# Strassen's algorithm in both products of two of three token blocks of a gated MoE layer, with stored operands

## The chip, the cores and the metric

The kernel runs on one core of a Trainium2 chip. The metric is the device time of one execution in microseconds, as the median of several runs. A core has a matrix engine (TensorE, PE in the profile; its weight loads are PEld), three engines for elementwise work (VectorE or DVE, ScalarE or ACT, GpSimd or POOL) and SyncE (SP), whose queue issues all DMA transfers here.

## What is computed

Linear attention over 4 batches of 576 tokens and 8 heads gives 2304 tokens of 512 features. They pass a dense layer (512 to 2048 to 512) and then four experts, all of which see every token:

```python
def _moe_ref(x, w_in, w_out):
    h = x @ w_in
    g = np.maximum(0.01 * h, h)
    return g @ w_out

def _moe2_ref(x, domain_probs, w1, w2):
    p = domain_probs / (domain_probs.sum(-1, keepdims=True) + 1e-09)
    out = np.zeros((N, D))
    for e in range(E):                       # 4 experts, w1[e] 512x1024, w2[e] 1024x512
        h = np.maximum(x @ w1[e], 0.0)
        out += p[:, e:e + 1] * (h @ w2[e])
    return out
```

All arrays are fp32.

## The kernel before

Each fp32 factor is split in a high part of a shorter type (fp32r) and the remainder; a product is three matmuls, hi·hi, hi·lo and lo·hi (`PASS`). ScalarE makes most high parts, VectorE or GpSimd subtract them for the low parts.

The attention of batch b+1 runs between the matmuls of the first layer for batch b. For the first layer VectorE splits weights and activations (`gt<-g,gt`, `wt`, L118) and adds the results up in `acc` (L551). SyncE loads the probabilities early (`load_probs`, L133) among the attention's first loads; VectorE normalises them in place (L138).

The second layer takes the tokens in NB = 3 blocks of 768 (two halves of TH = 384) and the 4096 hidden units of the four experts in NC2 = 16 chunks of 256: 48 groups, one call of `group(k)` each. A group has two parts:

- The up product of chunk k is a 2x2 block product by the Strassen-Winograd scheme: 7 products (`product`, matmul L722) of 6 matmuls with 384 columns, on sums of the weights (AOPS) and of the tokens (XOPS). They accumulate in the banks X, V and Y; two sums on VectorE (V += s1 at L824, Z = Y + s0 at L827) put the four quarters together, and ScalarE (L735) and VectorE (L739) apply the relu and split.
- The down product of chunk k−1 is conventional: six token tiles (`down`, matmul L761), each of 6 matmuls with 512 columns. VectorE multiplies each by its token's probability and adds it to the output tile `ob` (L777). After the last chunk of a block the tile is stored (L781).

The order on TensorE within a group is products 1 and 5, tile 3, products 2 and 6, tile 4, products 3 and 7, tiles 5 and 0, product 4, tiles 1 and 2. `keep_in_program_order` (by `kept`) holds it.

The weights of a chunk are loaded anew for each block (`w2_dma`, `w2_dma_d`), one group ahead. GpSimd forms the four sums of w1 (`w2_sums`, L682), ScalarE rounds (L699, L710) and GpSimd subtracts (L704 twice a group, L714 once). The token sums of block 0 are made by `x2_steps(0)` on VectorE (L619, L642) at the end of the first layer, out of `acc` in SBUF; those of blocks 1 and 2 by GpSimd during the block before.

Of the kernel before, what the change touches and what calls it, by code (L numbers as in the profile page):

```python
# [7 lines left out]
F32 = mybir.dt.float32  # L8
# [8 lines left out]
DF = 128  # L17
# [7 lines left out]
GF = 4  # L25
# [46 lines left out]
N_X = 10  # L72
# [3 lines left out]
NC2 = NE * FF2 // 256  # L76


@with_exitstack
def body(ctx, tc, kT, qT, vh, w_phi, w_in, w_out, probs, w1, w2, out):  # L80
# [3 lines left out]
    xp = ec(tc.tile_pool(name="xp", bufs=N_X))  # L84
# [19 lines left out]
    def unit(name, dt=F32):  # L104
        return up.tile([128, S], dt, tag="u", name=name)
# [125 lines left out]
    def kv_side(b, hp, h):  # L231
# [17 lines left out]
        if h == 1:  # L249
            if "n" in DIRECT[b]:  # L250
                kv = up.tile([128, 4, 128], F32, tag="u", name="kv")
# [3 lines left out]
            kvh = up.tile([128, 4, 128], F32R, tag="u", name="kvh")  # L255
            kvl = up.tile([128, 4, 128], F32R, tag="u", name="kvl")
# [235 lines left out]
    accs = {}  # L492

# [83 lines left out]

    XOPS = ("b11", "t1", "b21", "t2", "b22", "t3", "t4")
    xops = {}

    def pieces(*halves):

        cuts = sorted({0, TH} | {S - t0 % S for t0 in halves if S - t0 % S < TH})  # L590
        return [
            (o, e - o, [((t0 + o) // S, (t0 + o) % S) for t0 in halves])
            for o, e in zip(cuts, cuts[1:])
        ]

    x2p = []

    def x2_steps(j):

        T = (2 * TH * j, 2 * TH * j + TH)  # L600
        kind = ([xp, xp, xp, 0, 0], [0, xp, xp, xp, xp], [xp, xp, xp, 0, 0])[j]
        slots, raw = [], []
        xops[j] = {}

        def half(i):
            if i % 3 == 0:
                pool = kind[i // 3] or x2p[0]
                slots.append(pool.tile([128, 3, 2, TH], F32R, tag="x", name="xo"))
            return slots[i // 3][:, i % 3]

        def part(d, t, o, n):
            b, s = t
            return accs[b][:, 2 * d : 2 * d + 2, s : s + n]

        eng = nc.vector if j == 0 else nc.gpsimd

        def diff(out, f, g, halves):
            for o, n, at in pieces(*halves):
                kept(eng.tensor_tensor(  # L619
                    out=out[:, :, o : o + n], in0=f(o, n, at), in1=g(o, n, at), op=ALU.subtract  # L620
                ))

        def step(i, name):
            if name[0] == "t":
                if not raw:
                    raw.append((x2p[0] if j else xp).tile([128, 3, 2, TH], F32, tag="x", name="xt"))
                r = raw[0][:, {"t1": 0, "t2": 1, "t3": 2, "t4": 0}[name]]
                of = {
                    "t1": (lambda o, n, at: part(0, at[1], o, n), lambda o, n, at: part(0, at[0], o, n), T),
                    "t2": (lambda o, n, at: part(1, at[0], o, n), lambda o, n, at: raw[0][:, 0, :, o : o + n], T[1:]),  # L630
                    "t3": (lambda o, n, at: part(1, at[0], o, n), lambda o, n, at: part(0, at[0], o, n), T[1:]),
                    "t4": (lambda o, n, at: part(1, at[0], o, n), lambda o, n, at: raw[0][:, 1, :, o : o + n], T[:1]),
                }[name]
                diff(r, *of)
                src = [(0, TH, r)]
            else:
                d, t = int(name[1]) - 1, T[int(name[2]) - 1]
                src = [(o, n, part(d, at[0], o, n)) for o, n, at in pieces(t)]
            hi, lo = half(2 * i), half(2 * i + 1)
            for o, n, r in src:  # L640
                kept(nc.scalar.copy(out=hi[:, :, o : o + n], in_=r))
                kept(eng.tensor_tensor(  # L642
                    out=lo[:, :, o : o + n], in0=r, in1=hi[:, :, o : o + n].bitcast(F32), op=ALU.subtract
                ))
            xops[j][name] = hi, lo
# [292 lines left out]
```

## Time and profile before

| | before |
|---|---|
| median of 3 runs | 1379.31 us (1379.19 to 1380.08) |
| the profiled execution: span | 1378.8 us |
| granted TensorE clock, mean | 0.992 |
| TensorE busy | 1352.1 us (98%) |
| VectorE busy | 817.8 us (59%) |
| ScalarE busy | 657.9 us (48%) |
| GpSimd busy | 567.8 us (41%) |
| DMA traffic | 134.94 MB, mean 98 GB/s |

The span is the time from the first to the last instruction of one profiled execution; the runs are timed without a profile. Busy time is summed over an engine's instructions; that of TensorE is modelled at the ends of its matmuls, so distances between starts are more reliable than durations there. A row of a timeline gives the start, the duration, engine, line, operation, output<-input and how many instructions it joins; behind it in brackets stands the idle time ahead of it and what ended it.

### The profile page before, as it was taken

What the parts mean: (1) busy time and instruction counts of PE and PEld (TensorE: products, weight loads), DVE (VectorE), ACT (ScalarE), POOL (GpSimd) and SP (SyncE); (2) the same over time, 40 slices, a digit from 0 to 9 for tenths busy, and PEclk for the clock granted to TensorE, in tenths of its full rate; (3) what the DMA queues carried; (4) which work ended last, traced back from release to release, by engine and by line L of the source; (5) the groups of instructions that cost most, each with busy time, mean ns of one, the idle gap of its engine ahead of it and who ended that gap; (6) DMA issues with size and microseconds to landing.
All of it is one profiled execution on the core that took longest, in us unless ns stands there. A gap on an engine that the chain in (4) does not pass through costs nothing.

```text
span 1378.8 us, 21301 instructions
## 1 busy us (share of the span) xinstructions
PE 1352.1 (98%) x8105; PEld 1262.2 (92%) x8105; DVE 817.8 (59%) x1285; ACT 657.9 (48%) x1201; POOL 567.8 (41%) x398
## 2 busy tenths in 40 slices
PE   8979999999999999999999999999999999999998
PEld 6778999999999999998999999999999999899997
DVE  4589999678786656553555445445454444554444
ACT  5657657676576435424343443434443343433331
POOL 3211102111111000027767666767767675565651
PEclk9989999999999999999999999999999999999999
DMA  6466645333332222302212122321121232122111
GB/s 220 113 217 234 220 167 166 111 120 105 109 103 66 75 86 73 104 24 94 75 61 77 62 68 71 107 77 62 62 77 62 77 107 77 62 64 76 61 62 62
DMA packets 78518, 134.94 MB, mean 98 GB/s; under 512 B 12240, under 2 KB 22608, under 8 KB 78416
## 3 DMA queue, kind: packets, MB, share of 16 engines
q1 hardware_dynamic: 78416, 133.58, 29.8%
q8 instruction: 64, 1.05, 0.3%
q14 instruction: 38, 0.31, 0.1%
HBM read 120.30 MB, written 13.18 MB: 97 GB/s over the span
## 4 chain that ended last, share of the span: by engine, by line
PE 95%; DVE 1%; DMA 1%; issue 1%; ACT 1%; POOL 1%; SPq 0%; POOLq 0%; ACTq 0%; DVEq 0%
PE po L761 29%; PE hp L506 15%; PE op L538 14%; PE py L722 11%; PE pv L722 7%; PE px L722 7%; PE kvp L242 5%; PE nm L335 4%; PE pk L204 2%; PE pq L292 1%; PE pq L289 1%; DMA qraw<-qT 1%; POOL wul L704 0%; DMA r<-w 0%; DMA ds<-nf 0%
## 5 line engine op out<-in xcount | busy, mean ns | idle before, releaser
L761 PE MATMUL po<-wd,gh 128*128 128x512 f32 x1152 | 387.7, 391 | 0.9 <-POOL wd L714 0.9
L777 DVE SCALAR_TENSOR_TENSOR ob<-po,pe,ob 128x512 f32<-128x512 f32 x270 | 201.6, 749 | 216.6 <-PE po L761 216.6
L761 PEld LDWEIGHTS po<-wd,gh 128*128 128x128 f32 x1152 | 216.6, 188 | 42.3 <-POOL wd L714 1.3
L761 PE MATMUL po<-wd,gl 128*128 128x512 f32 x576 | 226.2, 393 | 0.0
L538 PE MATMUL op<-gt,wt 128*128 128x288 f32 x1536 | 219.9, 297 | 1.5 <-DVE gt L118 0.8
L296 POOL PARTITION_ALL_REDUCE mb<-pc x32 | 72.3, 2266 | 355.7 <-ACT pc L294 294.7
L506 PE MATMUL hp<-xh,wt 128*128 128x288 f32 x1024 | 216.2, 298 | 0.0
L538 PEld LDWEIGHTS op<-gt,wt 128*128 128x128 f32 x1536 | 207.9, 188 | 2.9 <-DVE gt L118 1.0
L506 PEld LDWEIGHTS hp<-xh,wt 128*128 128x128 f32 x1024 | 167.5, 188 | 1.0 <-ACT wt L117 0.3
L506 PE MATMUL hp<-xl,wt 128*128 128x288 f32 x512 | 151.8, 297 | 0.0
L714 POOL TENSOR_TENSOR wd<-r,wd 128x1024 fp32r<-128x1024 f32 x48 | 114.9, 2394 | 89.4 <-ACT wd L710 89.4
L722 PE MATMUL py<-xo,wuh 128*128 128x384 f32 x576 | 148.3, 339 | 0.7 <-DVE pz L827 0.7
L682 POOL TENSOR_TENSOR rs<-r 128x256 f32<-128x256 f32 x96 | 71.1, 741 | 188.8 <-DMA r<-w 188.8
L704 POOL TENSOR_TENSOR wul<-rs,wuh 128x1024 fp32r<-128x1024 f32 x48 | 115.5, 2406 | 65.9 <-ACT wuh L699 65.9
L704 POOL TENSOR_TENSOR wul<-r,wuh 128x768 fp32r<-128x768 f32 x48 | 88.8, 1851 | 85.7 <-ACT wuh L699 85.7
L761 PEld LDWEIGHTS po<-wd,gl 128*128 128x128 f32 x576 | 108.2, 188 | 15.2
L722 PEld LDWEIGHTS py<-xo,wuh 128*128 128x128 f32 x576 | 104.9, 188 | 4.6 <-DVE pz L827 1.0
L722 PE MATMUL px<-xo,wuh 128*128 128x384 f32 x384 | 98.9, 338 | 0.7 <-DVE acc L551 0.7
L722 PE MATMUL pv<-xo,wuh 128*128 128x384 f32 x384 | 99.1, 339 | 0.0
L722 PE MATMUL py<-xo,wul 128*128 128x384 f32 x288 | 97.3, 338 | 0.0
L506 PEld LDWEIGHTS hp<-xl,wt 128*128 128x128 f32 x512 | 96.3, 188 | 0.4
L807 ACT COPY py<-px 128x384 f32<-128x384 f32 x48 | 22.2, 463 | 143.4 <-PE px L722 137.3
(114 smaller groups left out, 2349.9 us busy)
## 6 DMA issues: line engine op xcount, KB each, us to landing
r<-w SPq DMA_DIRECT2D x192, 256.0 KB, 2.8
wr<-w SPq DMA_DIRECT2D x96, 256.0 KB, 2.7
qraw<-qT SPq DMA_DIRECT2D x32, 288.0 KB, 3.7
r<-w_out SPq DMA_DIRECT2D x9, 1024.0 KB, 9.0
r<-w_in SPq DMA_DIRECT2D x8, 1024.0 KB, 6.2
w<-w SPq DMA_DIRECT2D x32, 256.0 KB, 2.8
v<-vh SPq DMA_DIRECT2D x16, 480.0 KB, 4.0
kraw<-kT SPq DMA_DIRECT2D x16, 288.0 KB, 4.0
```

Source lines behind the costliest of these rows:

```text
L204: nc.tensor.matmul(o, lhsT=x[:, cs], rhs=w, start=(i == 0), stop=(i == len(P) - 1))
L242: nc.tensor.matmul(kvp[:, a * 128 : (a + 1) * 128], lhsT=lhs, rhs=v[:, c, h * D : h * D + 128], start=(c == 0), stop=(c == 4),)
L296: nc.gpsimd.partition_all_reduce(mb, pc, 128, bass_isa.ReduceOp.absmax)
L335: nc.tensor.matmul(o, lhsT=a[:, 2 * (h % 2) + j], rhs=x[:, j * HS : (j + 1) * HS], start=(j == 0 and i == 0), stop=(j == 1 and i == len(P) ...
L506: nc.tensor.matmul(hp[:, n, 0:HS], lhsT=wi[:, a, kk * 128 : (kk + 1) * 128], rhs=x[z][:, kk, n * HS : (n + 1) * HS], start=(kk == 0 and i ...
L538: nc.tensor.matmul(op[:, n, 0:HS], lhsT=wt1[1, C * GF + f][:, a, d * 128 : (d + 1) * 128], rhs=gts[C * GF + f][:, z, n * HS : (n + 1) * HS ...
L682: kept(nc.gpsimd.tensor_tensor(out=o, in0=x, in1=y, op=op))
L704: kept(nc.gpsimd.tensor_tensor(out=lo[:, at], in0=(r[:, 1:4], s)[i], in1=hi[:, at].bitcast(F32), op=ALU.subtract))
L714: kept(nc.gpsimd.tensor_tensor(out=d[:, 1], in0=r2, in1=d[:, 0].bitcast(F32), op=ALU.subtract))
L722: kept(nc.tensor.matmul(out, lhsT=ws[w][:, AOPS[a], kk * 128 : (kk + 1) * 128], rhs=xo[z][:, kk], start=first and n == 0, stop=n == 5, ski ...
L761: kept(nc.tensor.matmul(op, lhsT=(gh, gl)[z][:, 2 * f + t, q : q + 128], rhs=d[:, w, f], start=n == 0, stop=n == 5,))
L777: kept(nc.vector.scalar_tensor_tensor(out=o, in0=op, scalar=ps, in1=o, op0=ALU.mult, op1=ALU.add))
```

## The change

Block 1 of the change's name is the first block (k = 0 to 15), blocks 2 and 3 are k = 16 to 47. The first block keeps its products, their order and its output form, and stores its operands to DRAM: the split w1 sums (`wu`), the split quarters of w2 (`wp`), and sums of w2 (`wx`), which are new: VectorE adds them (`ws_sums`, four operations of 128x256 per group) and subtracts their high parts (`ws_lo`), ScalarE rounds. In all 3.67 MB are stored per group.

```diff
     def w2_lo(k, r, s, i):
...
+        if i:
+            d = drw.tile([128, 7, 2, 256], F32, name=f"wu_{k}")
+            for z, t in ((0, hi), (1, lo)):
+                nc.sync.dma_start(out=d[:, :, z], in_=t.bitcast(F32))
+            wd[0, k] = {n: d[:, q] for q, n in enumerate(AOPS)}
...
+            (2, r2[:, 2], r2[:, 0], ALU.subtract),
+            (3, r2[:, 3], s[:, 1], ALU.subtract),
+        ):
+            kept(nc.vector.tensor_tensor(out=s[:, o], in0=x, in1=y, op=op))
...
+    def ws_lo(k):
+        hi, lo = wsd.pop(k)
+        h, s = hi.bitcast(F32), lo.bitcast(F32)
+        kept(nc.vector.tensor_tensor(out=lo, in0=s, in1=h, op=ALU.subtract))
+        t = drw.tile([128, 4, 2, 256], F32, name=f"wx_{k}")
+        for z, x in ((0, h), (1, s)):
+            nc.sync.dma_start(out=t[:, :, z], in_=x)
...
     def group(k, r, r2, fill):
...
         product(k, 2, X, False)
         relu_hi(k, 0, X)
         relu_lo(k, 0, X)
+        ws_sums(k, r2)
         product(k, 6, Y, False)
```

The output of the first layer is stored to DRAM (`x2_0` to `x2_3`) and loaded again by `x2_steps`, whose elementwise work is now all GpSimd's, 11 operations of 128x768 for a block, with 7 ScalarE roundings. For the first and second block it runs during the last batch of the first layer (`spread(x2_steps(0), B - 0.95, B - 0.5) + spread(x2_steps(1), B - 0.5, B - 0.05)`), for the third in twelve chunks of the second block.

The probabilities are laid out expert by expert and, once normalised, also stored transposed, so that `p_load` can fetch a row of them to all partitions:

```diff
+        pT.append(drw.tile([NE, NTOK], F32, name="pT"))
+        nc.sync.dma_start(out=pT[0].rearrange("e (c p) -> p e c", p=128), in_=pe)
```

The second and third block are written as a list of steps with times (`moe2_plan`, 14 units a chunk). Up products of chunk k and down products of chunk k−1 alternate, seven each. The hidden layer is kept with hidden units on partitions and tokens on columns, gated by the probabilities at once (`gate`), and the down product takes the same seven-product scheme: four differences on GpSimd (`gsum`), seven roundings on ScalarE (`ghi`), seven subtractions on GpSimd (`glo`), 7 × 6 matmuls of 384 columns, each product added to its own accumulator `ac` of 128x768 (`evict`). Operands come by 14 loads of 256 KB per chunk (`w_load`), issued nine to eleven products ahead. After the last chunk of a block seven additions between accumulators (`plus`) give the four output quarters, which are stored transposed.

```diff
+    def down_product(k, p):
+
+        i, a, b = DOWN[p]
+        t = po[k, i] = m2["po"].tile([128, 2, 512], F32, tag="o", name="po")
+        w, g = wo[1, k, a], go[k, b]
+        for m in range(2):
+            for n, (wz, z) in enumerate(PASS):
+                kept(nc.tensor.matmul(
+                    t[:, m, 0:TH],
+                    lhsT=w[:, wz, m * 128 : (m + 1) * 128],
+                    rhs=g[:, z],
...
+    def evict(k, p):
...
+            kept(nc.vector.tensor_tensor(out=A[j, i], in0=src, in1=A[j, i], op=ALU.add))
...
+                for p in range(7):
+                    at(B + 2 * p, up_product, k, p)
...
+                for p in range(7):
+                    at(B + 2 * p + 1, down_product, k - 1, p)
+                    at(B + 2 * p + 2.0, evict, k - 1, p)
+            if k > KA + 1 and k % NC2 == 1:
+                j = k // NC2 - 1
+                for t, a, b in ((2.2, 2, 1), (4.2, 6, 1), (6.2, 7, 6), (8.2, 6, 5),
+                                (10.4, 5, 7), (12.2, 3, 6), (14.2, 4, 7)):
+                    at(B + t, plus, V, j, a, b)
...
+        for t, e, a, b in (
+            (6.2, V, 6, 1), (4.2, V, 3, 5), (2.2, V, 2, 1), (6.4, V, 3, 6), (8.2, V, 7, 6),
+            (8.3, G, 4, 7), (8.4, V, 5, 7),
+        ):
+            at(B + t, plus, e, j, a, b)
```

The scheduler decides where instructions outside `kept` stand. At three places the order is as follows. The first is SyncE's queue at the program's start (`qraw` and `kraw` are the attention's queries and keys, `w_in` and `w_out` the first layer's weights). Before:

```order
L133 DMA pe<-probs 128x72
L166 DMA qraw<-qT 128x576 x2
L154 DMA kraw<-kT 128x576
L166 DMA qraw<-qT 128x576 x3
L445 DMA r_207<-w_in 128x2x1024
L445 DMA r_209<-w_out 128x2x1024
```

After, in the same place:

```order
L142 DMA pe<-probs 128x72
L181 DMA qraw<-qT 128x576 x2
L169 DMA kraw<-kT 128x576
L181 DMA qraw<-qT 128x576
L153 DMA pT<-pe 128x72x1
L181 DMA qraw<-qT 128x576 x2
L460 DMA r_210<-w_in 128x2x1024
L460 DMA r_212<-w_out 128x2x1024
```

The store of the probabilities, which waits for VectorE, now stands ahead of two query loads and of the first weights.

The second is VectorE in one group of the first block (`gl` the relu's low part, `ob` an eviction, `pv` and `pz` the two sums). Before:

```order
L739 SCALAR_TENSOR_TENSOR gl<-px,gh 128x384
L777 SCALAR_TENSOR_TENSOR ob<-po,pe,ob 128x512
L824 TENSOR_TENSOR pv<-pv,s 128x384
L827 TENSOR_TENSOR pz<-py,s 128x384
L739 SCALAR_TENSOR_TENSOR gl<-pv,gh 128x384
L739 SCALAR_TENSOR_TENSOR gl<-pz,gh 128x384
```

After (`wsl` are the sums of w2, `r_7632` is w2 as loaded):

```order
L794 TENSOR_TENSOR wsl<-wsl,wsh 128x1024
L869 SCALAR_TENSOR_TENSOR ob<-po,pe,ob 128x512
L831 SCALAR_TENSOR_TENSOR gl<-px,gh 128x384
L783 TENSOR_TENSOR wsl<-r_7632 128x256
L783 TENSOR_TENSOR wsl<-wsl,r_7632 128x256
L783 TENSOR_TENSOR wsl<-r_7632 128x256
L783 TENSOR_TENSOR wsl<-r_7632,wsl 128x256
L869 SCALAR_TENSOR_TENSOR ob<-po,pe,ob 128x512
L918 TENSOR_TENSOR pv<-pv,s 128x384
L921 TENSOR_TENSOR pz<-py,s 128x384
```

Four sums now stand between the relu step of X and the eviction and the two sums behind it, and one subtraction of 128x1024 earlier.

The third is the end of VectorE's queue. Before:

```order
L739 SCALAR_TENSOR_TENSOR gl<-py,gh 128x384
L777 SCALAR_TENSOR_TENSOR ob<-po,pe,ob 128x512 x8
```

After, from the last gate on:

```order
L984 SCALAR_TENSOR_TENSOR b_15192<-py,pb 128x384
L1029 TENSOR_TENSOR ac<-po,ac 128x768 x2
L1032 TENSOR_TENSOR ac<-ac 128x768
L1029 TENSOR_TENSOR ac<-po,ac 128x768
L1032 TENSOR_TENSOR ac<-ac 128x768
L1029 TENSOR_TENSOR ac<-po,ac 128x768
L1032 TENSOR_TENSOR ac<-ac 128x768 x2
L1029 TENSOR_TENSOR ac<-po,ac 128x768
L1032 TENSOR_TENSOR ac<-ac 128x768 x2
L1029 TENSOR_TENSOR ac<-po,ac 128x768 x3
```

Six additions between accumulators stand between the eight last evictions; the seventh is on GpSimd.

## Rows read from the trace of the kernel before

**Rows 1.** The page: busy times, and the chain that ended last.

```profile
PE 1352.1 (98%) x8105; PEld 1262.2 (92%) x8105; DVE 817.8 (59%) x1285; ACT 657.9 (48%) x1201; POOL 567.8 (41%) x398
PE 95%; DVE 1%; DMA 1%; issue 1%; ACT 1%; POOL 1%; SPq 0%; POOLq 0%; ACTq 0%; DVEq 0%
```

**Rows 2.** TensorE's waits after 560 us, first and last of five: total, times, longest.

```profile
PE po L761 <- POOL wd L714: 0.9, 1, 0.9
...
PE py L722 <- DVE pz L827: 0.7, 1, 0.7
```

**Rows 3.** TensorE's timeline in the first block of the second layer.

```profile
645.11 0.39 PE L761 MATMUL po<-wd,gh 128*128 128x512 f32 x1
...
647.86 0.51 PE L722 MATMUL px<-xo,wuh 128*128 128x384 f32 x2
...
663.50 0.51 PE L722 MATMUL px<-xo,wuh 128*128 128x384 f32 x2
```

**Rows 4.** The timeline's end, all engines.

```profile
1374.59 0.39 PE L761 MATMUL po<-wd,gh 128*128 128x512 f32 x1
...
1375.02 0.75 DVE L777 SCALAR_TENSOR_TENSOR ob<-po,pe,ob 128x512 f32<-128x512 f32 x1 [0.61 <-PE po L761]
```

**Rows 5.** VectorE's groups by shape, 100 to 620 us: busy, mean ns, idle before.

```profile
L642 DVE TENSOR_TENSOR xo<-xt,xo 128x768 fp32r<-128x768 f32 x4 | 3.7, 950 | 1.0 <-ACT xo L641 1.0
...
L619 DVE TENSOR_TENSOR xt<-acc 128x384 f32<-128x384 f32 x4 | 2.0, 552 | 0.0
```

**Rows 6.** GpSimd's groups by shape, whole span.

```profile
L619 POOL TENSOR_TENSOR xt<-acc,xt 128x768 f32<-128x768 f32 x3 | 5.5, 1840 | 0.0
...
L619 POOL TENSOR_TENSOR xt<-acc 128x384 f32<-128x384 f32 x2 | 2.0, 1014 | 0.0
```

**Rows 7.** One line of VectorE from 500 to 600 us; then timelines of VectorE and GpSimd.

```profile
L118 DVE TENSOR_TENSOR gt<-g,gt 128x576 fp32r<-128x576 f32 x16 | 12.1, 759 | 2.3
...
610.67 1.87 DVE L118 TENSOR_TENSOR gt<-g,gt 128x576 fp32r<-128x576 f32 x1 [0.74 <-ACT gt L117]
...
609.52 2.41 POOL L704 TENSOR_TENSOR wul<-rs,wuh 128x1024 fp32r<-128x1024 f32 x1
```

**Rows 8.** Timelines of TensorE and GpSimd in the second layer's first group.

```profile
622.49 0.62 PE L722 MATMUL px<-xo,wuh 128*128 128x384 f32 x2 [0.68 <-DVE acc L551]
...
628.05 1.83 POOL L704 TENSOR_TENSOR wul<-r,wuh 128x768 fp32r<-128x768 f32 x1
629.83 2.42 POOL L704 TENSOR_TENSOR wul<-rs,wuh 128x1024 fp32r<-128x1024 f32 x1
```

**Rows 9.** Timelines of TensorE, VectorE and GpSimd in a later group.

```profile
882.42 0.52 PE L722 MATMUL px<-xo,wuh 128*128 128x384 f32 x2
...
887.68 0.56 DVE L739 SCALAR_TENSOR_TENSOR gl<-px,gh 128x384 fp32r<-128x384 f32 x1 [0.82 <-ACT gh L735]
...
886.08 1.85 POOL L704 TENSOR_TENSOR wul<-r,wuh 128x768 fp32r<-128x768 f32 x1 [2.57 <-ACT wuh L699]
889.72 2.41 POOL L704 TENSOR_TENSOR wul<-rs,wuh 128x1024 fp32r<-128x1024 f32 x1 [1.79 <-ACT wuh L699]
...
894.23 0.51 PE L722 MATMUL py<-xo,wuh 128*128 128x384 f32 x2
```

**Rows 10.** The start: SyncE, ScalarE, one transfer's landing, and a stretch of small packets.

```profile
10.80 0.38 SPq L445 DMA_DIRECT2D r<-w_in  x1
...
25.37 1.22 ACT L460 ACTIVATE w<-r 128x512 f32<-128x512 f32 x2
...
r<-w_in SPq DMA_DIRECT2D x8, 1024.0 KB, 6.2
...
35.50:35.75 0.25, 0.25 (x5) 0.25 (x4) 0.25 (x1) 0.25 (x2) 0.00 (x0) 1.00 0.37 19
```

**Rows 11.** DMA: the page's queue row, and a stretch (last columns clock, DMA share, GB/s).

```profile
q1 hardware_dynamic: 78416, 133.58, 29.8%
...
100.00:200.00 100.00, 98.10 (x688) 93.17 (x687) 94.52 (x166) 70.31 (x142) 9.84 (x4) 1.00 0.64 226
```

More of the change, by code (lines that the diff above doesn't have):

```diff
@@ L576, in moe1_group @@
         return M
[L585 to L645, printed above, removed]
-        return [lambda i=i, name=name: step(i, name) for i, name in enumerate(XOPS)]
@@ new lines, in body, with xo_load, w_load @@
+    xo = {}
+    def xo_load(m):
+        j, i = divmod(m, 7)
+        name = XOPS[i]
+        pool, tag = (m2["te"], "te") if m % N_XO < N_XE else (m2["tx"], "tx")
+        hl = [pool.tile([128, 2, TH], F32R, tag=tag, name="xo2") for _ in range(2)]
+        for z in range(2):
+            kept(nc.sync.dma_start(out=hl[z].bitcast(F32), in_=xod[j][name][:, z]))
+        xo[j, name] = hl
+    wo = {}
+    def w_load(i, n):
+        k, p = divmod(n, 7)
+        k += KA
+        name = (UP, DOWN)[i][p][1]
+        if i:
+            pool, tag = (m2["w2e"], "w2e") if n % N_W2 < N_W2E else (m2["w2"], "w2")
+        else:
+            pool, tag = m2["w1"], "w1"
+        t = pool.tile([128, 2, 256], F32R, tag=tag, name="wo")
+        kept(nc.sync.dma_start(out=t.bitcast(F32), in_=wd[i, k % NC2][name]))
+        wo[i, k, name] = t
@@ L812, in group @@
             w2_lo(k + 1, r, s, 0)
+        if k:
+            ws_lo(k - 1)
         run(down(k - 1, 3))
@@ L840, in group, with p_load, up_product @@
         run(down(k - 1, 2))
+    pb = {}
+    def p_load(j, e):
+        t = m2["p"].tile([128, 2, TH], F32, tag="p", name="pb")
+        src = pT[0][e : e + 1, 2 * TH * j : 2 * TH * (j + 1)]
+        kept(nc.sync.dma_start(
+            out=t.rearrange("p a s -> p (a s)"), in_=src.to_broadcast([128, 2 * TH])
+        ))
+        pb[j, e] = t
+    banks = {}
+    gr, go, sv = {}, {}, {}
+    def up_product(k, p):
+        i, a, b = UP[p]
+        if i == 1:
+            banks["x"] = m2["px"].tile([128, 512], F32, tag="x", name="px")[:, 0:TH]
+        if i == 5:
+            banks["v"] = m2["pv"].tile([128, 512], F32, tag="v", name="pv")[:, 0:TH]
+        out = banks[{1: "x", 2: "x", 5: "v", 3: "v"}.get(i, "y")]
+        w, x = wo[0, k, a], xo[k // NC2, b]
+        first = i in (1, 5)
+        n = 0
+        for kk in range(2):
+            for wz, z in PASS:
+                kept(nc.tensor.matmul(
+                    out,
+                    lhsT=w[:, wz, kk * 128 : (kk + 1) * 128],
+                    rhs=x[z][:, kk],
+                    start=first and n == 0,
+                    stop=n == 5,
+                    skip_group_check=not first,
+                ))
+                n += 1
@@ new lines, in ftile, with save, gate, gsum @@
+    def ftile(name):
+        return m2["f"].tile([128, TH], F32, tag="f", name=name)
+    def save(k, name, bank):
+        sv[name] = ftile("s")
+        kept(nc.scalar.copy(out=sv[name], in_=banks[bank]))
+    def gate(k, name, src, h):
+        j, c = divmod(k, NC2)
+        t = gr[k, name] = ftile(name)
+        kept(nc.vector.scalar_tensor_tensor(
+            out=t, in0=src, scalar=0.0, in1=pb[j, c // (NC2 // NE)][:, h],
+            op0=ALU.max, op1=ALU.mult,
+        ))
+    def gsum(k, name, a, b):
+        t = gr[k, name] = ftile(name)
+        kept(nc.gpsimd.tensor_tensor(out=t, in0=gr[k, a], in1=gr[k, b], op=ALU.subtract))
@@ new lines, in evict, with plus, store @@
+    def evict(k, p):
+        i = DOWN[p][0]
+        j, c = divmod(k, NC2)
+        src = po.pop((k, i))[:, :, 0:TH]
+        if c == 0:
+            A[j, i] = m2["a"].tile([128, 2, TH], F32, tag="a", name="ac")
+            kept(nc.scalar.copy(out=A[j, i], in_=src))
+        else:
+            kept(nc.vector.tensor_tensor(out=A[j, i], in0=src, in1=A[j, i], op=ALU.add))
+    def plus(eng, j, a, b):
+        kept(eng.tensor_tensor(out=A[j, a], in0=A[j, a], in1=A[j, b], op=ALU.add))
+    def store(j, a, i, h):
+        t0 = 2 * TH * (j - 1) + TH * h
+        r = out[2 * TH * DM :].rearrange("(d s) -> d s", s=NTOK - 2 * TH)
+        nc.sync.dma_start(
+            out=r[i * 256 : (i + 1) * 256, t0 : t0 + TH].rearrange("(t p) s -> p t s", p=128),
+            in_=A[j, a],
+        )
```

379 lines of the change are left out of this document (293 added, 86 removed).

## The prediction

> **What bounds the kernel now.** I read the page first, then the chain of waits, then TensorE's own waits, then timelines of one group. The page gives TensorE 1352.1 of 1378.8 us and no other engine above 59%; the chain that ended last is 95% TensorE [rows 1]. The next view asks whether TensorE ever stands still in the second layer: after 560 us it waits five times, 0.7 to 0.9 us each, 3.8 us in all [rows 2]. So in this stage the time is the sum of its matmuls, and a change must be counted in matmuls first and in new waits second.
>
> Matmul records overlap, so I take the distance between starts. Two groups of the second layer start at 647.86 and 663.50: 15.64 us for 42 matmuls of 384 columns (seven products of six) and 36 of 512 (six token tiles of six). Twelve of the wide ones lie between 645.11 and 647.86: 0.229 us each, 8.25 us for 36. That leaves 7.39 us for the 42, 0.176 us each [rows 3].
>
> **What the change takes away.** In blocks 2 and 3 the 36 wide matmuls of a group become 42 of 384 columns: 7.39 in place of 8.25 us. A chunk is then 84 × 0.176 = 14.78 us, 0.86 us less. There are 32 such chunks: **−27.5 us**. A rule of the Trainium skill ("TensorE: Matmul & The Clock Gate", "Back-to-back issue gap") gives N/2.4 + 2.5 ns from start to start, by which 36 × 215.8 − 42 × 162.5 = 0.94 us would be saved per chunk and 30.2 us in all; the rows show some 14 ns over that on both widths, and I go by the rows.
>
> **What it adds.** Six places can make TensorE wait. Each is priced from the nearest rows, with both ends.
>
> *The end.* Today the last matmul starts at 1374.59, VectorE evicts it at 1375.02 in 0.75 us, and the last store ends the span at 1378.8 [rows 4]. Afterwards the last chunk has no up products between its down products: seven of 6 × 0.176 = 1.06 us follow each other in 7.4 us, and each needs an eviction of 128x768, then there are seven additions between accumulators. VectorE took 0.950 us for a 128x768 operation from SBUF [rows 5]; the additions are of that kind, and I take the same for the evictions. Its queue then holds 8 evictions (one left from the chunk before) and 6 additions, 14 × 0.95 = 13.3 us, 13.6 with its first semaphore, against 7.4 + 0.25 + 0.95 = 8.6 us if only the last product had to be evicted: 5.0 us. The seventh addition is GpSimd's, 1.84 us by its rows for that shape [rows 6], partly beside the others, and its store is larger. Taken **+6**, between 4 and 8. What covers today's evictions, the matmuls between them, is what is gone.
>
> *The border of blocks 2 and 3.* In one chunk VectorE has its four gates and two sums of 128x384, 6 × 0.56 = 3.4 us by a step of that width [rows 9], and seven additions of two SBUF operands, 6.7 us. That fits in 14.78. But GpSimd now has 11 subtractions of 128x384 a chunk at 1.01 us [rows 6], 11.1 us, and each addition may have to wait for one (below): 3.4 + 6.7 + 7 × 1.0 = 17.1, 2.3 us too long. Taken **+2**, 0 to 5.
>
> *GpSimd against VectorE.* At 610.67 a VectorE subtraction of 128x576 with both inputs in SBUF took 1.87 us, where the mean of its line is 0.759; a GpSimd operation ran from 609.52 to 611.93, and the slow one ended at 612.54, 0.61 us after it [rows 7]. The Trainium skill ("SBUF — State Buffer", "Who interferes with whom") says that such a VectorE instruction and a GpSimd one lock each other out; by that rule the pair behaves as these rows do. It does not touch operations with an operand in PSUM, which most of VectorE's here have.
>
> *The last block of the first layer.* The operands of blocks 1 and 2 are now made there, all on GpSimd: 22 operations of 128x768 at 1.84 us = 40.5 us [rows 6] in a stretch where VectorE's subtractions of SBUF pairs feed the matmuls. Each collision costs a VectorE step up to 1.1 us (1.87 − 0.76), mostly absorbed by operands made ahead, since TensorE hardly waits there now [rows 2]. Taken **+2**, 0 to 8.
>
> *The first groups.* Block 1 now has four VectorE sums of 128x256 per group, SBUF with SBUF. By VectorE's rows for 384 and 768 elements (0.552 and 0.950, 1.04 ns an element) one takes 0.42 us. In group 0, which starts at 622.49, GpSimd's two splits run back to back from 628.05 to 632.25 [rows 8], just where these sums come (5.8 us after the start, as next worked out): up to 3.9 us late, and the same once more before GpSimd's lead is back. Taken **+4**, 0 to 8.
>
> *The other groups of block 1.* In a settled group, which starts at 882.42, the sums stand behind the subtraction that ends at 888.24, 5.82 us in. GpSimd's first split ends at 887.93, its second starts at 889.72 [rows 9]. The last of four sums would start 1.26 us after 5.82, at 7.08, 0.22 us before the second split at 7.30. So they just fit, and a few will not. Taken **+3** over 14 groups, 0 to 8.
>
> *The start.* The gate probabilities are now stored transposed, 9216 elements of 4 bytes, 576 on each of 16 DMA engines. The packets of a window with only small ones kept the engines 0.37 × 0.25 us × 16 / 128 = 11.6 ns each [rows 10] (19 GB/s × 0.25 us is one store of 4.5 KB in 128 pieces), so 6.7 us; at the mean packet of the page, 0.298 × 16 × 1378.8 / 78416 = 84 ns [rows 11], 48 us. I take the first, since its packets are as small. In SyncE's queue the store stands ahead of two query loads and of the first expert weights, and waits for VectorE's quotient; the weights were issued at 10.80, landed 6.2 us later by the page, and are first read at 25.37 [rows 10], some 8 us of slack. Taken **+1**, 0 to 40.
>
> Everything else I cost at nothing: the loads of 256 KB and additions of blocks 2 and 3 stand nine to eleven products ahead of use, GpSimd has 11.1 to 13 us of work in a chunk of 14.78, ScalarE less. If those loads were late, TensorE would show waits on them.
>
> **Sum**, against the profiled span of 1378.8: −27.5 + 6 + 2 + 2 + 4 + 3 + 1 = −9.5, so 1369.3. The median of the runs, 1379.31, lies 0.5 above that span; I add it: **1369.8 us**.
>
> **Rivals.**
>
> *The gain comes nearly whole.* The costs of block 1 and of the start all have zero as one end; with 4 at the end and 0 to 2 at the border this gives 1379.3 − 27.5 + 4 to 6, 1356 to 1358. For it: TensorE waits so little today. Against: the end is a queue that I can count.
>
> *VectorE's sums lose to GpSimd in every group of block 1* (slower). The margin of 0.22 us is the point that decides. If the sums start only after the second split, at 889.72 + 2.41 = 892.13, they end at 893.8; behind them stand an eviction of 0.75 and the two sums of 0.57 that product 4 needs, ready at 895.7 and seen at 895.95. Product 4 starts at 894.23 today [rows 9], so TensorE waits 1.7 us, 27 us over 16 groups: 1369.8 + 27 − 7 (the terms it replaces) = 1390. Any wait above some 1.2 us a group ends slower than before. For it: rows 7 show the lock. Against: the sums come first, if barely, and are short.
>
> *The stores saturate the DMA engines in block 1* (slower at its upper end). Per group 3.67 MB are stored in pieces of 1 KB and 1.05 MB loaded: 302 GB/s, where 100 to 200 us shows 226 at a share of 0.64 [rows 11]. The page's mean packet is 133.58 MB / 78416 = 1.70 KB in 84 ns. 224 packets of 1 KB per engine take between 50 and 84 ns, 11 to 19 us, and the loads 3.2 more: 14 to 22 us against 15.64. From 55 ns on they fall behind; each further 5 ns costs 224 × 5 ns = 1.1 us a group, 18 us in 16 (1369.8 − 3 + 18 = 1385 at 60 ns, 1467 at 84 ns). Against: buffers let a store take a whole group, and the same 302 GB/s need only 0.86 of the engines at the efficiency of that stretch.
>
> *The transposed store holds up the start.* At 84 ns a packet the queries and first weights are 40 us late, less 8 of slack: 1385 to 1405.
>
> That the products would not be exchanged is excluded: the instruction counts are in the order of the program.
>
> **How the numbers follow.** Forecast 0.67 (1359 to 1377 by its bounds taken singly); whole gain 0.10; VectorE's sums late 0.08; DMA in block 1 0.10; slow start 0.05. A measurement of this kernel tells 0.2% (2.8 us) from no change. Faster holds the first two cases, less 0.02 for the forecast's upper tail, and a fifth of the DMA case: 0.77. Slower holds the sums and the start, 0.13, and half of the DMA case: 0.18. The rest, 0.05, is no change. The range of 8 in 10, 1355 to 1384, leaves out some 0.03 below and, above, what the three slow cases hold there, 0.17.
>
> **What would show it.** In the changed profile: a distance of 14.8 us from chunk to chunk in blocks 2 and 3; hardly a TensorE wait there, but 2 us in the second chunk of block 3; the last matmul some 10 us before the end in place of 4; in block 1 a period of 15.6 to 15.9 us, with waits in the first two groups named after VectorE; small packets done before 20 us. A period of over 16.5 us in block 1 would make the forecast wrong, by VectorE if its sums last over 1 us each, by DMA if a load lands last. So would a chunk above 15.2 us later on.

## The result and the profile after

The changed kernel takes 1391.28 us (median of 4 runs, 1388.83 to 1391.72) against 1379.25 us before: 1.008 times, 95% interval 1.0066 to 1.0094. It is slower by 12 us, where 1369.8 was forecast. One execution of one experiment (the sums moved, on the change) took 4633.78 us, with matmuls of 384 columns some 0.63 us apart at a granted clock of 1.00, and is left out of every time below.

| | before | after |
|---|---|---|
| span of the profiled execution | 1378.8 us | 1389.2 us |
| TensorE busy | 1352.1 us (98%) | 1332.2 us (96%) |
| VectorE busy | 817.8 us (59%) | 945.0 us (68%) |
| GpSimd busy | 567.8 us (41%) | 653.7 us (47%) |
| DMA traffic | 134.94 MB, 98 GB/s | 313.91 MB, 226 GB/s |
| mean granted clock | 0.992 | 0.982 |

TensorE has 20 us less work and a span that is 10 us longer, so it must wait some 30 us more than before. Its waits, over the whole span, longest first (total, times, longest):

```profile
PE pq L304 <- DMA qraw<-qT: 18.1, 3, 15.9
PE po L1013 <- issue: 6.4, 4, 2.3
PE py L811 <- DVE pz L921: 5.9, 1, 5.9
```

The first are query products of the attention, the longest wait of 15.9 us by the fifth of them; they wait for the queries (`qraw`). The second is in the last chunk, the third in the second layer's first group. Between 680 and 1354 us TensorE does not wait at all. To put a sum beside each, I take the starts of the first product at five borders: group 0, group 2, the first chunk of block 2, the last chunk, and the end. Before, group 0 and group 2 start at 622.49 [rows 8] and 647.86 [rows 3], the other two at:

```profile
866.82 0.52 PE L722 MATMUL px<-xo,wuh 128*128 128x384 f32 x2
...
1351.02 0.51 PE L722 MATMUL px<-xo,wuh 128*128 128x384 f32 x2
```

After, in TensorE's timeline:

```profile
644.76 0.51 PE L811 MATMUL px<-xo,wuh 128*128 128x384 f32 x2
...
675.85 0.51 PE L811 MATMUL px<-xo,wuh 128*128 128x384 f32 x2
...
894.16 1.05 PE L964 MATMUL px<-xo,wo 128*128 128x384 f32 x5
...
1353.86 0.87 PE L964 MATMUL px<-xo,wo 128*128 128x384 f32 x4
```

| stretch | before, us | after, us | difference | forecast |
|---|---|---|---|---|
| attention and first layer | 622.5 | 644.8 | +22.3 | +3 |
| groups 0 and 1 | 25.4 | 31.1 | +5.7 | +4 |
| the other 14 groups of block 1 | 219.0 | 218.3 | −0.7 | +3 |
| blocks 2 and 3 to the last chunk's start | 484.2 | 459.7 | −24.5 | −23.8 |
| last chunk and end | 27.8 | 35.3 | +7.5 | +4.3 |
| span | 1378.8 | 1389.2 | +10.4 | −9.5 |

(The first chunk of block 2 still has the conventional down product of chunk 15. So the forecast's column has 30 × −0.86 + 2 up to the last chunk's start, and the last two gains, −1.72, with the +6 of the end in the last line.) Of the 20 us between forecast and result, 19 are in the first line.

**The start.** SyncE's timeline of the changed kernel:

```profile
11.89 0.38 SPq L153 DMA_DIRECT2D pT<-pe  x1
12.31 19.72 SPq L181 DMA_DIRECT2D qraw<-qT  x2
32.07 0.43 SPq L460 DMA_DIRECT2D r<-w_in  x1
```

The store of the probabilities is issued at 11.89, and the two query loads behind it then occupy the queue for 19.72 us; the first weights, issued at 10.80 before [rows 10], follow at 32.07. TensorE meanwhile:

```profile
25.33 0.60 PE L219 MATMUL pk<-wraw,kraw 128*128 128x256 f32 x2
41.80 2.26 PE L304 MATMUL pq<-qraw,wraw 128*128 128x288 f32 x4 [15.87 <-DMA qraw<-qT]
```

The DMA view of the stretch from 11 to 45 us (KB each, us to landing):

```profile
qraw<-qT SPq DMA_DIRECT2D x3, 288.0 KB, 16.8
...
pT<-pe SPq DMA_DIRECT2D x1, 36.0 KB, 28.5
```

36 KB take 28.5 us to land. That is 49 ns for each of 576 pieces per engine, where I took 11.6. The windows (PE, PEld, DVE, ACT, POOL, clock, DMA share, GB/s) show DMA engines that are busy with hardly any bytes, and TensorE's granted clock, which falls from 1.00 to 0.50 (2.4 to 1.2 GHz) after it has stood idle:

```profile
22.00:24.00 2.00, 2.00 (x21) 2.00 (x20) 1.99 (x3) 1.24 (x2) 0.00 (x0) 1.00 1.94 1
...
30.00:32.00 2.00, 0.00 (x0) 0.00 (x0) 0.00 (x0) 0.00 (x0) 0.00 (x0) 0.50 1.27 1
```

The clock is still 0.50 when the queries are in: the four matmuls at 41.80 take 2.26 us, where the four of the query product before them, at 20.79, took 1.14.

**Groups 0 and 1.** VectorE's sums and GpSimd's splits in group 0, after; first VectorE's timeline, then GpSimd's:

```profile
650.06 0.75 DVE L783 TENSOR_TENSOR wsl<-r 128x256 f32<-128x256 f32 x1
650.85 0.84 DVE L783 TENSOR_TENSOR wsl<-wsl,r 128x256 f32<-128x256 f32 x1
651.61 2.02 DVE L783 TENSOR_TENSOR wsl<-r 128x256 f32<-128x256 f32 x1
653.56 2.56 DVE L783 TENSOR_TENSOR wsl<-r,wsl 128x256 f32<-128x256 f32 x1
...
656.50 0.55 DVE L921 TENSOR_TENSOR pz<-py,s 128x384 f32<-128x384 f32 x1
```

```profile
651.37 1.99 POOL L751 TENSOR_TENSOR wul<-r,wuh 128x768 fp32r<-128x768 f32 x1
653.31 2.52 POOL L751 TENSOR_TENSOR wul<-rs,wuh 128x1024 fp32r<-128x1024 f32 x1
```

The third sum ends 0.3 us after the first split, the fourth 0.3 us after the second; what would take 0.42 us takes 2.02 and 2.56, and TensorE waits 5.9 us for `pz`. Behind the wait its granted clock is 0.52, and 12 matmuls of 384 columns take 3.9 us instead of 2.1:

```profile
657.00:661.00 4.00, 3.89 (x12) 3.89 (x13) 2.12 (x5) 2.92 (x5) 2.41 (x2) 0.52 0.61 223
```

In a settled group of the same kernel the sums stand free:

```profile
712.76 0.41 DVE L783 TENSOR_TENSOR wsl<-r 128x256 f32<-128x256 f32 x1
...
713.88 0.42 DVE L783 TENSOR_TENSOR wsl<-r,wsl 128x256 f32<-128x256 f32 x1
```

The second split of that group starts at 714.31, 0.43 us after the last sum's start; 0.22 was forecast.

**Block 1 and the chunks.** A window of 150 us in block 1, columns as above:

```profile
700.00:850.00 150.00, 150.00 (x751) 135.15 (x750) 98.83 (x163) 66.75 (x106) 92.20 (x69) 1.00 0.97 326
```

The DMA engines are busy 0.97 of the time, and TensorE still does not wait. A chunk of block 2 takes 954.51 − 939.71 = 14.80 us (14.78 forecast):

```profile
939.71 0.51 PE L964 MATMUL px<-xo,wo 128*128 128x384 f32 x2
...
954.51 0.68 PE L964 MATMUL px<-xo,wo 128*128 128x384 f32 x3
```

**The end.** TensorE's timeline, then VectorE's:

```profile
1376.07 1.29 PE L1013 MATMUL po<-go,wo 128*128 128x384 f32 x6 [1.35 <-issue]
1379.70 1.29 PE L1013 MATMUL po<-go,wo 128*128 128x384 f32 x6 [2.34 <-issue]
1382.55 2.26 PE L1013 MATMUL po<-go,wo 128*128 128x384 f32 x6 [1.56 <-issue]
```

```profile
1375.03 0.94 DVE L1029 TENSOR_TENSOR ac<-po,ac 128x768 f32<-128x768 f32 x1
1376.00 2.72 DVE L1032 TENSOR_TENSOR ac<-ac 128x768 f32<-128x768 f32 x2
1378.65 0.95 DVE L1029 TENSOR_TENSOR ac<-po,ac 128x768 f32<-128x768 f32 x1
1379.63 1.95 DVE L1032 TENSOR_TENSOR ac<-ac 128x768 f32<-128x768 f32 x2
...
1384.91 0.96 DVE L1029 TENSOR_TENSOR ac<-po,ac 128x768 f32<-128x768 f32 x1 [1.60 <-PE po L1013]
```

Each product starts 0.1 us after an eviction ends (1375.97, 1379.60): with two bank pairs for `po`, TensorE waits for VectorE, whose evictions stand behind additions. The last product, behind the last of these waits, takes 2.26 us where those before took 1.29; the granted clock is 0.50 from 1382 to 1385 us.

### The profile page after: what moved, and what is told of

Read it like the earlier page. It is cut to its first block, busy times and chain, and to the rows that moved or that the text cites. A ratio compares the mean times of both kernels' runs of the same rounds, so it can differ in the third digit from the quotient of the medians.

```text
span 1389.2 us, 23190 instructions
## 1 busy us (share of the span) xinstructions
PE 1332.2 (96%) x8297; PEld 1284.6 (92%) x8297; DVE 945.0 (68%) x1381; ACT 643.3 (46%) x1228; POOL 653.7 (47%) x534
## 2 busy tenths in 40 slices
DMA packets 205794, 313.91 MB, mean 226 GB/s; under 512 B 29168, under 2 KB 104560, under 8 KB 205680
## 4 chain that ended last, share of the span: by engine, by line
PE 64%; POOL 12%; issue 9%; DMA 6%; DVE 5%; ACT 3%; SPq 0%; POOLq 0%; ACTq 0%; DVEq 0%
PE op L555 12%; PE hp L522 11%; PE po L851 10%; PE po L1013 7%; POOL go L999 7%; POOL t L991 5%; PE kvp L257 4%; PE py L811 4%; PE nm L350 3%; PE py L964 3%; PE px L811 2%; PE pv L811 2%; PE px L964 2%; DMA qraw<-qT 2%; PE pv L964 2%
## 5 line engine op out<-in xcount | busy, mean ns | idle before, releaser
L1029 DVE TENSOR_TENSOR ac<-po,ac 128x768 f32<-128x768 f32 x210 | 200.4, 955 | 128.6 <-PE po L1013 128.5
L1013 PE MATMUL po<-go,wo 128*128 128x384 f32 x1344 | 274.5, 339 | 6.5 <-issue 6.4
L1013 PEld LDWEIGHTS po<-go,wo 128*128 128x128 f32 x1344 | 239.5, 188 | 8.2 <-issue 7.9
L999 POOL TENSOR_TENSOR go<-t,go 128x384 fp32r<-128x384 f32 x128 | 136.8, 1081 | 20.0 <-ACT go L995 20.0
L851 PE MATMUL po<-wd,gh 128*128 128x512 f32 x384 | 130.0, 392 | 0.0
L964 PE MATMUL py<-xo,wo 128*128 128x384 f32 x576 | 117.2, 338 | 0.0
L999 POOL TENSOR_TENSOR go<-b,go 128x384 fp32r<-128x384 f32 x96 | 101.4, 1056 | 9.3 <-ACT go L995 9.3
L964 PEld LDWEIGHTS py<-xo,wo 128*128 128x128 f32 x576 | 102.5, 188 | 0.2
L869 DVE SCALAR_TENSOR_TENSOR ob<-po,pe,ob 128x512 f32<-128x512 f32 x90 | 67.3, 748 | 45.4 <-PE po L851 45.4
L126 DVE TENSOR_TENSOR wt<-wr,wt 128x512 fp32r<-128x512 f32 x96 | 74.1, 793 | 15.7 <-ACT wt L125 13.9
L851 PEld LDWEIGHTS po<-wd,gh 128*128 128x128 f32 x384 | 72.1, 188 | 13.5
```

Of the source, the lines that this page charges most:

```text
L126: nc.vector.tensor_tensor(out=lo, in0=src, in1=hi.bitcast(F32), op=ALU.subtract)
L851: kept(nc.tensor.matmul(op.rearrange("p (h m) -> p h m", h=2), lhsT=(gh, gl)[z][:, 2 * f + t, q : q + 128], rhs=d[:, w, f::2], start=n == ...
L869: kept(nc.vector.scalar_tensor_tensor(out=o, in0=op, scalar=ps, in1=o, op0=ALU.mult, op1=ALU.add))
L964: kept(nc.tensor.matmul(out, lhsT=w[:, wz, kk * 128 : (kk + 1) * 128], rhs=x[z][:, kk], start=first and n == 0, stop=n == 5, skip_group_ch ...
L999: kept(nc.gpsimd.tensor_tensor(out=t[:, 1], in0=gr[k, name], in1=t[:, 0].bitcast(F32), op=ALU.subtract))
L1013: kept(nc.tensor.matmul(t[:, m, 0:TH], lhsT=w[:, wz, m * 128 : (m + 1) * 128], rhs=g[:, z], start=n == 0, stop=n == 2,))
```

## Experiments

Theory A says that the 4-byte store costs the start. Its rival B puts the loss on the rest of what the change does before the second layer. The first three runs tell them apart.

**The store alone, in the kernel before.**

```diff
-    pe = cst.tile([128, NTOK // 128, NE], F32, name="pe")
+    pe = cst.tile([128, NE, NTOK // 128], F32, name="pe")
...
+        pT = drw.tile([NE, NTOK], F32, name="pT")
+        nc.sync.dma_start(out=pT.rearrange("e (c p) -> p e c", p=128), in_=pe)
```

> The kernel before, with only the normalised probabilities laid out by expert and stored transposed (9216 pieces of 4 bytes) as the change does it. Theory A (this store fills SyncE's queue and the DMA engines at the start, and the attention's queries come late): 1379 + 20 to 25 = 1399 to 1404 us, TensorE idle for some 15 us ahead of 42 us, waiting for qraw. Rival B (the loss of the first 650 us comes from the other parts of the change there: stores of the first layer's output, token operands on GpSimd): 1379 to 1382 us.

Measured: 1400.48 us, 1.0159 times the kernel before (1.0142 to 1.0176), 22 us more. Its waits begin with:

```profile
PE pq L291 <- DMA qraw<-qT: 17.9, 4, 15.6
```

Theory A's number and its wait. Rival B falls as the main cause. In the profiled run, the fastest of the four, group 0 starts at 639.86, 17.4 us later than before, against 22.3 in the change: some 5 us of the first line of the table do not show in this run.

**The same store, later.** The probabilities are copied into a tile of a pool that opens in the last batch of the first layer, and stored from there.

```diff
-        nc.sync.dma_start(out=pT[0].rearrange("e (c p) -> p e c", p=128), in_=pe)
+        late = m2["pt"].tile([128, NE, C], F32, tag="pt", name="late")
+        nc.vector.tensor_copy(late, pe)
+        nc.sync.dma_start(out=pT[0].rearrange("e (c p) -> p e c", p=128), in_=late)
...
+        m2["pt"] = opened(left, "pt", 1, side="right")
```

> The change, with the same 4-byte store issued in the last batch of the first layer, among weight loads, by way of a copy in a pool that opens there. Theory A: the 20.4 us at the start go; the store still keeps the DMA engines for some 20 us, but the loads there run ahead of use, so 1367 to 1373 us; where the weights are not far enough ahead, a wait of up to 20 us moves there and the time stays near 1388. Rival B: 1388 to 1392 us, the start as late as in the change.

Measured: 1375.63 us (1371.6 to 1378.97, 10 runs), 0.9976 times the kernel before (0.9963 to 0.9988). The start is repaired, and a part of the loss has moved: group 0 starts at 636.42, still 13.9 us later than before. TensorE's waits from 480 to 640 us, and the store in the DMA view of 495 to 560:

```profile
PE op L557 <- DVE g L538: 8.0, 1, 8.0
```

```profile
pT<-late SPq DMA_DIRECT2D x1, 36.0 KB, 26.6
```

It still takes 26.6 us to land, and one wait of 8.0 us stands in that stretch; the first layer has none of that length there in any other kernel here. It is the mechanism of the start over again. A weight load of the first layer stands behind the store in SyncE's queue and keeps it for 16.52 us, ScalarE waits 12.27 us for such a load, and VectorE's queue stands behind ScalarE's rounding:

```profile
512.95 16.52 SPq L452 DMA_DIRECT2D wr<-w  x1
...
539.01 0.62 ACT L125 CAST wt<-wr 128x512 fp32r<-128x512 f32 x1 [12.27 <-DMA wr<-w]
```

From 544 to 552 us, behind TensorE's wait, the granted clock is 0.50.

**A wide store.** Two matmuls against a unit matrix turn the 72 columns into rows of 128 tokens.

```diff
-        nc.sync.dma_start(out=pT[0].rearrange("e (c p) -> p e c", p=128), in_=pe)
+        eye = upool[0].tile([128, 128], F32, tag="u", name="eye")
+        nc.sync.dma_start(out=eye, in_=eyes)
...
+        for z in range(2):
+            nc.tensor.matmul(t, lhsT=ph[:, z].rearrange("p e c -> p (e c)"), rhs=eyr, start=z == 0, stop=z == 1)
+        ts = cst.tile([NE * C, 128], F32, name="ts")
+        nc.vector.tensor_copy(ts, t)
+        nc.sync.dma_start(out=pT[0].rearrange("e (c p) -> (e c) p", p=128), in_=ts)
```

> The change, with the probabilities transposed by two small matmuls in the last batch of the first layer and stored as 72 rows of 512 bytes. Theory A: 1391.3 - 20.4 to 24.5 = 1367 to 1371 us, and no wait near the store. If this and the late 4-byte store agree, the place of the store decides; if this one alone is fast, the size of its pieces. Rival B: 1388 to 1392 us.

Measured: 1362.53 us (1360.6 to 1363.76), 0.988 times the kernel before (0.9864 to 0.9896), 29 us less than the change. Group 0 starts at 622.77, as before the change (622.49):

```profile
622.77 0.51 PE L823 MATMUL px<-xo,wuh 128*128 128x384 f32 x2
...
653.50 0.51 PE L823 MATMUL px<-xo,wuh 128*128 128x384 f32 x2
```

So both the place of the store and the size of its pieces count: the later place brings group 0 from 644.76 to 636.42, and at that place the larger pieces bring it to 622.77. A wide store at the early place was not tried. The result is 4.5 us below the expected range; the run with a pad, below, says why.

**Another queue.** The same early 4-byte store, issued by ScalarE.

```diff
-        nc.sync.dma_start(out=pT[0].rearrange("e (c p) -> p e c", p=128), in_=pe)
+        nc.scalar.dma_start(out=pT[0].rearrange("e (c p) -> p e c", p=128), in_=pe)
```

> The change, with the 4-byte store issued at the same point of the program from ScalarE's DMA queue in place of SyncE's. Theory A1 (the small pieces fill SyncE's queue, so that the query loads behind them are not issued until 32 us): the queries are on time, the start is late by under 5 us, 1370 to 1376 us. Theory A2 (the DMA engines are busy with the pieces for some 20 us, whatever queue holds them): the start is still late by 15 to 20 us, 1385 to 1391 us.

Measured: 1381.38 us (10 runs), 1.0015 times the kernel before (1.0003 to 1.0027), between the two theories. The waits from 10 to 60 us begin with:

```profile
PE pq L304 <- DMA qraw<-qT: 11.0, 3, 9.4
```

The longest wait shrinks from 15.9 to 9.4 us, and group 0 starts at 637.12: 7.6 of the 22.3 us are gone. The queries that stood behind the store are now in time; the wait is for the next ones, issued at 22.07 while the pieces are under way (in this run the store took 32.6 us to land). SyncE's blocked queue is thus a part of the loss, and the larger part stays with the engines that carry the pieces.

**The sums of groups 0 and 1, moved.** Two runs made this edit, on the change and on the kernel with the wide store.

```diff
-        ws_sums(k, r2)
+        if k > 1:
+            ws_sums(k, r2)
...
         relu_lo(k, 3, Z)
+        if k < 2:
+            ws_sums(k, r2)
```

> The change, with VectorE's four sums of w2 in groups 0 and 1 moved behind the two sums that product 4 needs. Theory C (these sums meet GpSimd's two splits, and TensorE's wait of 5.9 us in group 0 is theirs): the wait goes, 1391.3 - 5 to 6 = 1385 to 1386 us, and the four sums take about 0.42 us each. Rival D (GpSimd itself is late in group 0, since the weights land 10 us after it is free, and VectorE waits in any order): 1390 to 1392 us, with a wait of similar length in group 0 or 1.

> The change, with the wide store of the run before (1362.5 us) and VectorE's sums of groups 0 and 1 moved behind the two sums that product 4 needs. Theory C: TensorE's wait of 5.7 us in group 0 goes, 1362.5 - 5 to 6 = 1356.5 to 1357.5 us. Rival D (GpSimd is late in group 0 by itself): 1361 to 1363 us.

Measured: on the change 1390.18 to 1394.26 us in three runs. On the wide store 1365.47 us, against 1362.53 without the edit. No gain. TensorE's waits from 624 to 660 us in the second:

```profile
PE px L823 <- ACT py L910: 2.4, 1, 2.4
...
PE py L823 <- DVE pz L934: 0.7, 1, 0.7
```

and the first two of the moved sums in VectorE's timeline:

```profile
633.15 1.98 DVE L795 TENSOR_TENSOR wsl<-r 128x256 f32<-128x256 f32 x1
635.16 2.48 DVE L795 TENSOR_TENSOR wsl<-wsl,r 128x256 f32<-128x256 f32 x1
```

The wait of 5.7 us for `pz` shrinks to 0.7, but the sums meet GpSimd's next operations just the same, and their rounding on ScalarE now holds up the copy that the next group's products need. Groups 0 and 1 take 33.0 us (624.70 to 657.68) in place of 30.7. Theory C as I had put it, that the place of the sums is the matter, falls; it had to be asked whether the sums themselves are.

**The sums of groups 0 and 1, left out.** On the wide store. The run leaves out the four sums of chunks 0 and 1, with their rounding, subtraction and store; chunks 0 and 1 of blocks 2 and 3 read the sums of chunk 2 instead.

```diff
-        ws_sums(k, r2)
+        if k > 1:
+            ws_sums(k, r2)
...
-        ws_hi(k)
+        if k > 1:
+            ws_hi(k)
...
-        if k:
+        if k > 2:
             ws_lo(k - 1)
```

> The change with the wide store, leaving out VectorE's sums of w2 for the first two chunks, their rounding, subtraction and store (chunks 0 and 1 of blocks 2 and 3 use the sums of chunk 2). Theory C (the sums themselves, by meeting GpSimd, cost the first two groups 5 us wherever they stand): groups 0 and 1 take 25.4 to 26 us as in the kernel before in place of 30.7, 1356.5 to 1358 us, and no wait of over 1 us there. Rival D (GpSimd is late there by itself, and a wait shows in any case): 1361 to 1363 us.

Measured: 1360.22 us (1357.5 to 1362.08), 0.9863 times the kernel before (0.9849 to 0.9876); the median lies between the two theories and the runs scatter by about the effect, so I read the stretch. From 622.81 to 648.79 it takes 26.0 us:

```profile
622.81 0.51 PE L823 MATMUL px<-xo,wuh 128*128 128x384 f32 x2
...
648.79 0.51 PE L823 MATMUL px<-xo,wuh 128*128 128x384 f32 x2
```

That is 4.7 us less than with the sums (30.7), out of the 5.4 by which this kernel's first two groups were longer than before (25.4). So the sums and what hangs on them cost it, at both of the places tried. Rival D falls, but for the last 0.6 us. The run doesn't part the sums from their rounding, subtraction and store; that the sums do it is read from the rows of group 0 above.

**A pad.** An unused tile of 1600 bytes per partition in the changed kernel, as much as the wide store's tiles take.

```diff
+    pad = cst.tile([128, 400], F32, name="pad")
+    nc.gpsimd.memset(pad, 0.0)
     pe = cst.tile([128, NE, NTOK // 128], F32, name="pe")
```

> The change, with an unused tile of 1600 bytes per partition ahead of the probabilities, so that every later tile of that side moves in SBUF by as much as in the run with the wide store. Theory P (the distance from matmul to matmul, 0.176 us in the change and 0.1735 with the wide store, depends on where the operands stand): the chunks of blocks 2 and 3 come at 14.57 in place of 14.80 us, 32 x 0.23 = 7.4 us, about 1384 us. Rival Q (it came with the early store or differs from execution to execution): 14.8 us and 1390 to 1392 us.

Measured: 1384.24 us (1380.78 to 1387.22), 1.0043 times the kernel before (1.0028 to 1.0059). A chunk of block 2 takes 964.57 − 949.99 = 14.58 us in place of 14.80:

```profile
949.99 0.69 PE L966 MATMUL px<-xo,wo 128*128 128x384 f32 x3
...
964.57 0.69 PE L966 MATMUL px<-xo,wo 128*128 128x384 f32 x3
```

Theory P's number: with nothing changed but where the tiles stand (and a memset of the pad), 84 matmuls take 0.22 us less. The other runs agree and speak against rival Q: 14.80 again with the other queue (946.81 − 932.01), 14.57 with the wide store (945.41 − 930.84), and a third value, 14.65, with the late store, which has a tile pool more (945.63 − 930.98). What about the place matters was not tried.

**Another end.** The last chunk's down product as eight plain products that add up in PSUM, four evictions, and the seven additions before and beside them.

```diff
+    def down_last(k, q):
...
+            for a, b in (ab[0:2], ab[2:4]):
+                for wz, z in PASS:
+                    kept(nc.tensor.matmul(
+                        t[:, m, 0:TH],
...
-            (6.2, V, 6, 1), (4.2, V, 3, 5), (2.2, V, 2, 1), (6.4, V, 3, 6), (8.2, V, 7, 6),
-            (8.3, G, 4, 7), (8.4, V, 5, 7),
+            (-7.8, V, 6, 1), (-5.8, V, 7, 6), (-5.6, V, 6, 5), (0.1, V, 3, 6), (0.3, V, 5, 7),
+            (0.2, G, 2, 1), (2.5, V, 4, 7),
```

> The change, with another end: the down product of the last chunk by eight plain products that add up in four quarters, four evictions in place of seven, and the seven additions between accumulators before and beside them. Theory E (the end is VectorE's queue of 14 operations, by which TensorE's last products wait for their banks): last product about 8.5 us after the last up product instead of 17, no wait of over 0.5 us in it, 1391.3 - 7 to 9 = 1382 to 1384 us. Rival F (the end waits for GpSimd's last low parts, or for the stores): 1388 to 1391 us.

Measured: 1385.19 us (1382.39 to 1388.98), 1.0051 times the kernel before (1.0034 to 1.0069). In TensorE's waits of the last chunk the four of 6.4 us are replaced by two:

```profile
PE po L1047 <- DVE ac L1060: 1.3, 1, 1.3
PE py L969 <- DVE z L1107: 1.3, 1, 1.3
```

Theory E in kind, short of its range by 1 us: from the last chunk's start to the end it takes 31.0 us in place of 35.3. Two additions stood ahead of the sum `z`, and two more ran beside GpSimd's:

```profile
1368.18 3.67 DVE L1063 TENSOR_TENSOR ac<-ac 128x768 f32<-128x768 f32 x2
```

**Wide store and another end together**, with all seven additions on VectorE and two of them moved behind `z` (the edit is against the run before):

```diff
-            (-7.8, V, 6, 1), (-5.8, V, 7, 6), (-5.6, V, 6, 5), (0.1, V, 3, 6), (0.3, V, 5, 7),
-            (0.2, G, 2, 1), (2.5, V, 4, 7),
+            (-7.8, V, 6, 1), (-1.9, V, 7, 6), (-0.9, V, 6, 5), (2.05, V, 3, 6), (2.2, V, 5, 7),
+            (4.2, V, 4, 7), (4.3, V, 2, 1),
```

> The change with the wide store (1362.5 us) and the other end of the run before, in which six additions stand on VectorE behind the last gates' inputs and none on GpSimd. Theory E: the end falls by the 4.5 us that the run before showed from the last chunk's first product to the last eviction, and by about 1 us for the two additions that no longer hold up a sum: 1362.5 - 5 to 6 = 1356 to 1358 us. Rival F (with the operations out of each other's way the end is bound by the stores): 1358 to 1361 us.

Measured: 1356.49 us (1354.35 to 1357.47, 5 runs), 0.9836 times the kernel before (0.9822 to 0.9849): 22 us faster than the kernel before and 35 faster than the change. In the last chunk one wait of 0.8 us is left.

## Why the prediction was wrong

The sign came out wrong through one term, *the start*, "Taken +1, 0 to 40". Its mechanism was the one that I had listed as a rival with 0.05, "the transposed store holds up the start", and what that rival said of the price, "1385 to 1405", holds the result, though it reckoned with 84 ns a piece and 32 us at the start. The step that failed is the duration of a piece: I had two ends, 11.6 ns from a window with 36-byte packets [rows 10] and 84 ns from the page's mean packet [rows 11], and chose the low end "since its packets are as small". Measured are 49 ns, between the two. The window counted how long the engines are busy with packets in a short store; it did not show how fast a store of thousands of pieces of 4 bytes goes on. There the share was 0.37 at 19 GB/s; in the changed kernel it is 1.94 at 1 GB/s. Why a piece takes 49 ns stays open. The second slip was the slack. I counted 8 us for the first weights and did not ask for that of the queries, which stood in the same queue just behind the store. TensorE needs them first, and its loss there is 20.4 us (the attention's first output matmul, L350, starts at 46.88 us, before at 26.48). Of these, 2.0 are lost ahead of the long wait, 16.0 in it and 2.4 behind it, at the clock of 0.50; the forecast had no term for the clock.

Point by point, the other terms:

- **The gain.** 0.86 us a chunk was forecast, 15.64 to 14.78. Blocks 2 and 3 take 24.5 us less to the last chunk's start, where 23.8 was forecast. That was luck in part. The chunks came at 14.80 and 14.78 in this layout of SBUF and at 14.58 with the pad, which the forecast's 0.176 us a matmul could not know. And the border cost nothing that shows, where I took 2: the seven additions took 0.95 to 1.79 us each, VectorE still had the time, and the chunk in which they ran took 14.78 us, the next 14.83. The rule of the Trainium skill beside this term ("TensorE: Matmul & The Clock Gate", "Back-to-back issue gap") is given there for an isolated matmul, so its 0.94 us was no price for this stream.
- **The groups 0 and 1.** +4 forecast, +5.7 measured, by the mechanism of [rows 7] and all in one wait of group 0; what was missing is the clock behind it, 3.9 us for 12 matmuls instead of 2.1. The Trainium skill ("SBUF — State Buffer", "Who interferes with whom") says that a VectorE instruction with two SBUF inputs and GpSimd's reading of SBUF lock each other out; the trace agrees, with 2.56 us for a sum of 0.42.
- **The other groups of block 1.** +3 forecast, −0.7 measured. In every group from 2 to 15 the sums took 0.41 to 0.43 us, and the rival that VectorE's sums lose to GpSimd in all of them falls.
- **The stores.** The engines did come to 0.97 busy and 326 GB/s, and nothing waited. The rival's price per group was never paid.
- **The end.** +4.3 forecast with the gain of two chunks, +7.5 measured. The count of 14 operations on VectorE was right; what was missing is that the products wait for banks which these operations free, so that the last product came late too, and that additions took longer beside GpSimd, two of them 2.72 us together.
- **The last batch of the first layer.** +2 forecast. In the change 22.3 − 20.4 = 1.9 us more were lost between the start and group 0, but not there: from 480 us to group 0 TensorE waits for nothing, where the kernel before had three waits of 2.2 us together. They were lost earlier, in the batches before; which part of the change did it was not followed.

## What to carry to other kernels

A transfer is priced by its number of pieces, and where the trace has no transfer of that count and size, the term's upper end belongs in the forecast as soon as something on the critical path stands behind it in the queue. Ask of each moved or added DMA which loads follow it in its queue, and when TensorE needs the first of them, not the largest. A gain that was counted right in the steady state (24.5 us here) can be more than lost where the cover of other work is missing: 22.3 us at the start, 5.7 in the first groups and 7.5 at the end. And a long wait of TensorE costs more than its length: price the matmuls behind it at the granted clock that the rows show there.

## What was not expected of the hardware

- 9216 pieces of 4 bytes took 25.7 to 32.6 us to land in every kernel here that has this store, at two places of the program and from two queues.
- While they went, two query loads of 288 KB kept SyncE's queue for 19.72 us in place of the 2.94 us for three of them before; behind the late store one weight load kept it for 16.52 us.
- A pad of 1600 bytes moved the distance between matmuls of 384 columns from 0.176 to 0.1735 us, 7 us over blocks 2 and 3, with the granted clock at 1.00 in both.
- Behind waits of 15.9, 8.0 and 5.9 us TensorE's granted clock was 0.50 to 0.52 for some us.
- At a DMA share of 0.97 and 326 GB/s TensorE's loads of the second layer still came in time.
